# Recurrent attention and routed experts on one core: setup of the first two units in another order

## The chip, the cores and the metric

The kernel runs on one core of a Trainium2 chip. The metric is the device time of one execution in microseconds (us); where several executions are given, it is their median. The core's engines are TensorE (PE in the profile, PEld for its weight loads), VectorE (DVE), ScalarE (ACT), GpSimd (POOL) and SyncE (SP, which here issues the DMAs from and to HBM). Each engine takes its own instructions in the order in which they are written, and waits on semaphores that other engines or DMAs raise.

## The reference

Two stages: a recurrent attention over 4 batches, 8 heads, 768 tokens and head dimension 48, and a layer of 8 experts that takes its 3072 tokens of 384 features, each token going to the one expert with the highest logit.

```python
for t in range(S):                       # attention, per batch and head
    kt, vt, rt = k[:, :, t], v[:, :, t], r[:, :, t]
    cur = np.einsum('bhd,bhe->bhde', u[None] * kt, vt)
    y[:, :, t] = np.einsum('bhd,bhde->bhe', rt, state + cur)
    state = w[None, :, :, None] * state + np.einsum('bhd,bhe->bhde', kt, vt)
...
logits = x @ w_gate + modality_bias[modality_id]      # experts, x is y in token order
e_idx = np.argmax(logits, axis=1)
...
for e in range(E):
    mask = e_idx == e
    h = np.maximum(x[mask] @ w1[e], 0.0)
    out[mask] = gate_w[mask, None] * (h @ w2[e])
```

## The kernel before, in words

The tokens of the attention are cut into 24 units of 128 tokens: 6 chunks of each of the 4 batches, chunk by chunk. Within a unit the recurrence is written as products: with powers of the decay w, the scores of a token against the earlier tokens of its unit are (decayed r) times (decayed keys). For unit i the kernel computes

- `kc`, the keys turned to features by tokens, times powers of w (`keys`, L384), on VectorE;
- `rc`, r times powers of w (`decay`, L359), on GpSimd;
- `rk`, r times the keys, for the bonus u (`own_turned`, L377, on VectorE for units 0 to 3; `own_keys`, L371, on GpSimd later);
- the scores `psc` from `kc` and `rc`, 32 small products on TensorE (`scores`, L424), masked to `at` by VectorE (`causal`, L430);
- `pd`, which for unit 0 is called `psd`, from `rk` and u (`bonus`, L393), copied to `d` (`taken`, L398), and from it `dv` on ScalarE (`own`, L410);
- `kt`, the keys times the last powers (`carry`, L366), on GpSimd, for the state that later chunks take;
- the output `py` and the state's part `pst` on TensorE (`values`, L461 and L474).

r and k come turned from HBM into four buffers `ud`, the keys and values in token order into five buffers `kv`. For units 1 to 12 only r comes turned, and TensorE turns the keys itself (`keys_turned`, L347, tile `pkT`); for these units VectorE reads the keys from PSUM. For unit 0 VectorE reads keys and r from `ud`, in SBUF. The first 16 rows of `ud` are padding and must be blank.

`setup` (L82) prepares unit 0 and part of units 1 and 2 before the loop over the units begins, in an order written out by hand, engine by engine: blanks; the first DMAs; 10 products on constants (`pwarm`); the identity, the mask and counters (`counts`, L245: `base` and `line` are the counters' copies); the powers `pw`, `powk`, `powr`; `w128`, the 128th power; then `rc`, `kc` and `rk` of unit 0, the scores of unit 0, and `wtok`. For `wtok` ScalarE scales `powk` by `w128` (`wk`, L169), TensorE turns the four tiles (`pwk`, L176) and ScalarE copies the result (L177). `kt` needs `wtok`.

Two functions set what follows. `run` (L1090) goes through the units in a loop of steps; step i calls the functions above for the units around i, and a small table (`plan`) hangs further work at the end of a step. `pace` (L350) makes SyncE wait for a value of a running unit before it issues the next unit's transfers.

Of the kernel before, what the change touches and what calls it, by code (L numbers as in the profile page):

```python
# [9 lines left out]
F32 = mybir.dt.float32  # L10
# [50 lines left out]
LOW, TOP = 64 - D, 64 + D  # L61
# [3 lines left out]
class _Kernel:  # L65
# [16 lines left out]
    def setup(self):  # L82

        nc, c = self.nc, self.c
        w = c.tile([P, NPR], F32, name="w")
        nc.vector.memset(w, 1.0)
        nc.sync.dma_start(w[LOW:TOP, :], self.wT.rearrange("j d a -> (j d) a"))
        uT = c.tile([P, NPR], F32, name="uT")
        self.ud = [c.tile([P, 2 * NPR * P], F32, name=f"ud{q}") for q in range(4)]
        self.kv = [c.tile([P, LOW + 2 * DM], F32, name=f"kv{q}") for q in range(5)]  # L90
        self.kt = [c.tile([P, NPR, TOP], F32, name=f"kt{q}") for q in range(4)]
        self.st = [c.tile([P, B, NPR, 2 * D], F32, name=f"st{q}") for q in range(2)]
        zero = c.tile([P, P // 2], F32, name="zero")
# [4 lines left out]
        for t in self.kv:  # L98
            nc.vector.memset(t[:, :LOW], 0.0)
        nc.vector.memset(self.ud[0][:LOW], 0.0)  # L100
        nc.gpsimd.memset(self.ud[1][:LOW], 0.0)
        H2 = P // 2
        blank = lambda t: nc.scalar.copy(t.rearrange("p (a z) -> p a z", z=P // 2), zero[: t.shape[0]].unsqueeze(1).to_broadcast([t.shape[0], t.shape[1] // (P // 2), P // 2]))
        wb, one0, pw = (c.tile([P, NPR, H2 + 1], F32, name=n) for n in ("wb", "one0", "pw"))
        nc.vector.memset(wb, 0.0)
        nc.vector.memset(one0, 0.0)
        nc.vector.memset(one0[:, :, 0:1], 1.0)
        nc.vector.memset(uT, 0.0)
        blank(self.ud[2][:LOW])
        self.turned(0)  # L110
        self.turned(1)
        nc.sync.dma_start(uT[LOW:TOP, :], self.u.rearrange("o (a z) -> z (o a)", a=NPR))
# [35 lines left out]
        powk = self.powk = c.tile([P, NPR, P], F32, name="powk")  # L148
# [3 lines left out]
        nc.scalar.copy(self.powr[:, :, H2:], pw[:, :, :H2])  # L152
        nc.scalar.copy(self.powr[:, :, :H2], powk[:, :, : H2 - 1 : -1])
        self.w128 = c.tile([P, NPR], F32, name="w128")
        p64 = pw[:, :, H2 : H2 + 1].rearrange("p a o -> p (a o)")
        nc.vector.tensor_mul(self.w128, p64, p64)
        self.ub, self.uw = (c.tile([P, NPR, 2], F32, name=n) for n in ("ub", "uw"))
        self.decay(0, NPR, NPR // 2)
        self.keys(0, 2)
        u = self.ctx_[0]  # L160
        nc.vector.tensor_mul(u["rc"][:TOP, NPR // 2 :], u["rT"][:TOP, NPR // 2 :], self.powr[:TOP, NPR // 2 :])
        self.own_turned(0)
        self.decay(1)
        self.scores(0)
        self.wtok = c.tile([P, NPR, 2 * D], F32, name="wtok")
        wk = []
        for pr in range(NPR):
            t = self.a.tile([P, P], F32, tag="wk", name=f"wk{pr}", bufs=4)
            nc.scalar.activation(t, powk[:, pr, :], AF.Copy, scale=self.w128[:, pr : pr + 1])  # L169
            wk.append(t)  # L170
        blank(self.ud[3][:LOW])
        for t in self.kt:
            nc.scalar.copy(t[:, :, :LOW], zero[:, : NPR * LOW].rearrange("p (a z) -> p a z", a=NPR))
        pt = self.ps_y.tile([P, 512], F32, tag="y", name="pwk")
        for pr in range(NPR):
            nc.tensor.transpose(pt[:, pr * P : (pr + 1) * P], wk[pr], id32)  # L176
        nc.scalar.copy(self.wtok, pt.rearrange("p (a z) -> p a z", a=NPR)[:, :, LOW:TOP])  # L177
        blank(self.st[1].rearrange("p b a e -> p (b a e)"))
        nc.gpsimd.memset(self.ub, 0.0)
        for j, r in enumerate(HALVES):  # L180
            nc.gpsimd.tensor_copy(self.ub[r, :, j], uT[r])
        self.keys_turned(1)
        self.causal(0, 0)
        self.causal(0, 1)
        self.keys(1)
        self.own_turned(1)
        self.carry(0)
        self.decay(2)
        nc.gpsimd.tensor_mul(self.uw, self.ub, w.unsqueeze(2).to_broadcast([P, NPR, 2]))
        pst = self.ps_s.tile([P, 512], F32, tag="s", name="psd")  # L190
        self.bonus(0, pst)
        self.taken(0)
        self.carry(1)
        self.feed(3)
        self.turned(4)

# [48 lines left out]
    def counts(self):  # L245

        c, v = self.c, self.nc.gpsimd
        self.onesb = c.tile([P, P], BF16, name="onesb")
        v.memset(self.onesb, 1.0)
        self.id16 = c.tile([P, P], F16, name="id16")  # L250
        make_identity(self.nc, self.id16)
        self.tok = c.tile([P, NT // P], I32, name="tok")
        v.iota(self.tok, pattern=[[P, NCH], [S, B]], base=0, channel_multiplier=1)
        ii = c.tile([P, 3, E], I32, name="idxi")
        for q, (step, base) in enumerate(((1, 0), (-1, E), (CAP, 0))):
            v.iota(ii[:, q], pattern=[[step, E]], base=base, channel_multiplier=0)
        ci = c.tile([P, 3, E], F32, name="idxf")
        v.tensor_copy(ci, ii)
        self.idx, self.rev, self.cbase = (ci[:, q] for q in range(3))
        self.base = c.tile([P, E], F32, name="base")  # L260
        v.tensor_copy(self.base, self.cbase)
        self.line = c.tile([P, 1], F32, name="line")
        v.tensor_copy(self.line, self.tok[:, 0:1])

    def setup5(self):
        nc, c = self.nc, self.c
# [823 lines left out]
    def run(self):  # L1090
        nc, tc, m = self.nc, self.tc, self.m
# [25 lines left out]
        def plan(step, f):  # L1117
            at.setdefault(step, []).append(f)
# [70 lines left out]
        for i in range(NU - 1):  # L1189
# [304 lines left out]
```

## Time and profile before

| | us |
|---|---|
| three runs | 353.38, 355.96, 357.29 |
| median | 355.96 |
| the profiled execution | 353.3 |
| its span, first to last instruction | 351.5 |
| TensorE busy in it | 330.6 (94%) |
| VectorE, ScalarE, GpSimd busy | 220.0, 179.5, 154.6 |

A timeline row gives the start from the span's first instruction, the duration, the engine, the line of the kernel, the operation, what it writes and reads, and in brackets how long the engine sat idle before it and what ended that. Consecutive instructions of one kind stand in one row with their number, and its duration then runs from the first one's start to the last one's end. Instructions of one engine overlap slightly: the next starts some 0.05 to 0.1 us before the end of the one before.

### The profile page before, as it was taken

How to read it: one execution, taken by the hardware profiler on the slowest of the kernel's cores; microseconds unless marked ns; L12 is line 12 of the kernel's file. 1: busy time of each engine (PE TensorE's matmuls, PEld its weight loads, DVE VectorE, ACT ScalarE, POOL GpSimd, SP SyncE). 2: the span in 40 equal slices, each digit the busy share in tenths (PEclk: the TensorE clock that was granted, in tenths of full speed). 3: DMA queues.
4: the chain of work that ended last, by engine and by line, in shares of the span. 5: the costliest groups of instructions: out<-in, count | busy, mean ns of one | idle time of the engine just before them, and what ended most of it. 6: DMA issues, size and time to landing. Idle time of an engine off the chain costs nothing. (4 is left out here: it accounts for less than half of the span.)

```text
span 351.5 us, 15420 instructions
## 1 busy us (share of the span) xinstructions
PE 330.6 (94%) x5555; PEld 269.6 (77%) x5555; DVE 220.0 (63%) x740; ACT 179.5 (51%) x476; POOL 154.6 (44%) x230
## 2 busy tenths in 40 slices
PE   7999998969899997999999999998999999999993
PEld 3888898868768885978888777776778888777771
DVE  6878898799898956498458843348423332334850
ACT  7678776867957644667542222247222224553820
POOL 8888678776646762435265711112111120121221
PEclk9999999878999998999999999999999999999999
DMA  6767677999539998736334632116722111112110
GB/s 194 214 157 166 141 174 214 319 263 211 138 112 195 265 208 235 173 103 122 92 92 137 229 118 64 45 45 207 224 53 59 45 45 45 45 45 67 35 45 5
DMA packets 56798, 46.96 MB, mean 134 GB/s; under 512 B 42920, under 2 KB 50359, under 8 KB 56496
## 3 DMA queue, kind: packets, MB, share of 16 engines
q1 hardware_dynamic: 53552, 36.86, 44.2%
q0 software_dynamic: 3200, 9.47, 7.7%
q8 instruction: 31, 0.51, 0.7%
q14 instruction: 15, 0.12, 0.1%
HBM read 26.03 MB, written 11.83 MB: 108 GB/s over the span
## 5 line engine op out<-in xcount | busy, mean ns | idle before, releaser
L997 PEld LDWEIGHTS <-whi 128*128 128x128 f16 x1248 | 72.4, 98 | 3.6 <-issue 0.9
L1067 PEld LDWEIGHTS <-hh 128*128 128x128 f16 x416 | 38.7, 98 | 29.5 <-ACT hh L1001 3.1
L997 PE MATMUL phb<-mxT,whi 128*128 128x128 f16 x768 | 50.7, 219 | 0.0
L410 ACT ACTIVATE dv<-kv,d 128x48 f32<-128x48 f32 x172 | 43.1, 324 | 2.3 <-POOL gap L664 1.8
L1001 ACT ACTIVATE hh<-phb 128x256 f16<-128x256 f32 (+1 forms) x48 | 21.4, 453 | 32.6 <-PE L997 16.9
L997 PEld LDWEIGHTS <-wlo 128*128 128x128 f16 x624 | 37.7, 98 | 0.0
L371 POOL TENSOR_TENSOR rk<-rc,kc 112x512 f32<-112x512 f32 x20 | 25.7, 1286 | 25.0 <-DVE ebx L309 12.0
L430 DVE TENSOR_TENSOR at<-psc,mask 128x512 f32<-128x512 f32 x48 | 31.7, 682 | 6.0 <-PE psc L424 6.0
L1006 DVE SCALAR_TENSOR_TENSOR hl<-phb,hh 128x256 f16<-128x256 f32 (+1 forms) x48 | 24.1, 511 | 17.5 <-ACTq L1424 15.0
L1087 DVE TENSOR_SCALAR fac<-mt,wf 128x1 f32<-128x1 f32 x17 | 3.6, 213 | 49.1 <-ACTq L1424 36.1
L359 POOL TENSOR_TENSOR rc<-ud,powr 112x512 f32<-112x512 f32 (+1 forms) x25 | 31.1, 1248 | 3.6 <-DMA ud<-in_pd 2.6
L966 POOL TENSOR_TENSOR seenb<-otb,putb 128x1 int32<-128x1 int32 x16 | 3.0, 188 | 65.1 <-ACTq L1424 53.2
L1067 PEld LDWEIGHTS <-hl 128*128 128x128 f16 x208 | 19.8, 99 | 14.7 <-issue 2.4
L424 PE MATMUL psc<-rc,kc 64*64 64x128 f32 (+1 forms) x768 | 29.7, 294 | 1.4 <-POOL rc L359 0.7
L957 ACT ACTIVATE otb<-po,fac 128x384 f32<-128x384 f32 x16 | 9.2, 578 | 41.8 <-PE phb L997 41.8
L665 POOL DMA_INDIRECT rows<-row,posi x24 | 24.9, 1039 | 10.4 <-DVE pr L742 3.3
L1067 PE MATMUL po<-whi,hh 128*128 128x384 f16 x136 | 28.3, 327 | 1.1 <-ACT hh L1001 1.0
L997 PE MATMUL phb<-mxT,wlo 128*128 128x128 f16 x384 | 29.3, 219 | 0.0
L1067 PE MATMUL po<-wlo,hh 128*128 128x384 f16 x136 | 28.0, 326 | 1.3 <-DVE wlo L943 1.3
L424 PEld LDWEIGHTS psc<-rc,kc 64*64 64x64 f32 (+1 forms) x768 | 22.9, 143 | 7.9 <-issue 2.7
L943 DVE SCALAR_TENSOR_TENSOR wlo<-raw,ws,whi 128x1024 f16<-128x1024 f32 (+1 forms) x20 | 27.0, 1389 | 1.2 <-ACT whi L938 1.2
L997 PE MATMUL phs<-mxT,whi 128*128 128x128 f16 x432 | 27.2, 219 | 0.0
(272 smaller groups left out, 663.4 us busy)
## 6 DMA issues: line engine op xcount, KB each, us to landing
kv<-in_pt SPq DMA_DIRECT2D x21, 384.0 KB, 5.5
raw<-in_w SPq DMA_DIRECT2D x12, 512.0 KB, 4.7
ud<-in_pd SPq DMA_DIRECT2D x12, 384.0 KB, 6.0
raw<-in_w SPq DMA_DIRECT2D x2, 1536.0 KB, 6.4
ud<-in_pd SPq DMA_DIRECT2D x12, 192.0 KB, 2.7
rows<-pad SPq DMA_DIRECT2D x10, 193.0 KB, 3.1
kv<-in_pt SPq DMA_DIRECT2D x6, 192.0 KB, 3.7
rows<-row,posi POOLq DMA_INDIRECT x24, 4.5
```

What stands on the lines that cost most here:

```text
L359: nc.gpsimd.tensor_mul(u["rc"][:TOP, s], u["rT"][:TOP, s], self.powr[:TOP, s])
L371: nc.gpsimd.tensor_mul(u["rk"][:TOP], u["rc"][:TOP], u["kc"][:TOP])
L410: nc.scalar.activation(u["dv"][:, sl], u["v"][:, sl], AF.Copy, scale=u["d"][:, h : h + 1])
L424: nc.tensor.matmul(u["ps"][j][s, pr * P : (pr + 1) * P], u["kc"][r, pr, s], u["rc"][r, pr, :], start=True, stop=True)
L430: nc.vector.tensor_mul(u["at"][:, j * NPR : (j + 1) * NPR, :], u["ps"][j].rearrange("p (q t) -> p q t", q=NPR), self.mask.unsqueeze(1).to_ ...
L665: i = nc.gpsimd.indirect_dma_start(out=self.rows, out_offset=bass.IndirectOffsetOnAxis(ap=u["posi"][:, b : b + 1], axis=0), in_=u["row"][: ...
L943: self.nc.vector.scalar_tensor_tensor(self.wlo[:, sl], self.raw[:, sl], sc, self.whi[:, sl], ALU.mult, ALU.subtract)
L957: self.nc.scalar.activation(ot, po[:, :DM], AF.Copy, scale=gf[:, t : t + 1])
L997: self.nc.tensor.matmul(ph[:, q * P : (q + 1) * P], w[:, c0 : c0 + P], self.xT[:, xq, t * P : (t + 1) * P], start=i == q == 0, stop=i == l ...
L1001: self.nc.scalar.activation(self.hh[:, f0 : f0 + fb, t * P : (t + 1) * P], p3, AF.Relu)
L1006: self.nc.vector.scalar_tensor_tensor(self.hl[:, f0 : f0 + fb, r], p3, 0.0, self.hh[:, f0 : f0 + fb, r], ALU.max, ALU.subtract)
L1067: self.nc.tensor.matmul(po[:, :DM], h[:, f, t * P : (t + 1) * P], w[:, c0 : c0 + DM], start=first, stop=last)
```

## The change

In `setup`:

- `rk` of unit 0 moves from VectorE to GpSimd, as GpSimd's first product.
- `rc` of unit 0, of which GpSimd did the first two quarters and VectorE the second half, is now all VectorE's. VectorE does keys and decayed r in two halves, in turn, and `w128` after them.
- GpSimd's copies to `base` and `line` leave the setup for step 3 of the loop (`settle_counts`).
- The blanks of the buffers `ud1` to `ud3` are halved; the other halves are done by GpSimd at the ends of steps 5, 6 and 7 (`blank_rest`). ScalarE's blank of `ud3` is early now; its blanks of `kt` come ahead of `wk`, the blank of the state ahead of the copy to `wtok`.
- TensorE turns unit 1's keys ahead of `pwk`. Unit 0's bonus is written earlier, and its copy to `d` stands ahead of `rk` of unit 1 on VectorE.
- On GpSimd `rc` of unit 2 stands ahead of `kt` of units 0 and 1.
- The blank of `uT` is VectorE's second instruction instead of one behind the other blanks.

```diff
@@ setup
         uT = c.tile([P, NPR], F32, name="uT")
+        nc.vector.memset(uT, 0.0)
...
-        nc.gpsimd.memset(self.ud[1][:LOW], 0.0)
+        nc.gpsimd.memset(self.ud[1][:LOW, : NPR * P], 0.0)
...
-        nc.vector.memset(uT, 0.0)
-        blank(self.ud[2][:LOW])
+        for q in (2, 3):
+            blank(self.ud[q][:LOW, : NPR * P])
...
+        self.ub, self.uw = (c.tile([P, NPR, 2], F32, name=n) for n in ("ub", "uw"))
+        u = self.ctx_[0]
...
+        nc.gpsimd.tensor_mul(u["rk"][:TOP], u["kT"][:TOP], u["rT"][:TOP])
+        for q in range(2):
+            prs = slice(q * NPR // 2, (q + 1) * NPR // 2)
+            nc.vector.tensor_mul(u["kc"][:TOP, prs], u["kT"][:TOP, prs], powk[:TOP, prs])
+            nc.vector.tensor_mul(u["rc"][:TOP, prs], u["rT"][:TOP, prs], self.powr[:TOP, prs])
         p64 = pw[:, :, H2 : H2 + 1].rearrange("p a o -> p (a o)")
         nc.vector.tensor_mul(self.w128, p64, p64)
-        self.ub, self.uw = (c.tile([P, NPR, 2], F32, name=n) for n in ("ub", "uw"))
-        self.decay(0, NPR, NPR // 2)
-        self.keys(0, 2)
-        u = self.ctx_[0]
-        nc.vector.tensor_mul(u["rc"][:TOP, NPR // 2 :], u["rT"][:TOP, NPR // 2 :], self.powr[:TOP, NPR // 2 :])
-        self.own_turned(0)
         self.decay(1)
         self.scores(0)
         self.wtok = c.tile([P, NPR, 2 * D], F32, name="wtok")
+        for t in self.kt:
+            nc.scalar.copy(t[:, :, :LOW], zero[:, : NPR * LOW].rearrange("p (a z) -> p a z", a=NPR))
         wk = []
...
-        blank(self.ud[3][:LOW])
-        for t in self.kt:
-            nc.scalar.copy(t[:, :, :LOW], zero[:, : NPR * LOW].rearrange("p (a z) -> p a z", a=NPR))
+        blank(self.st[1].rearrange("p b a e -> p (b a e)"))
+        self.keys_turned(1)
         pt = self.ps_y.tile([P, 512], F32, tag="y", name="pwk")
...
-        blank(self.st[1].rearrange("p b a e -> p (b a e)"))
...
-        self.keys_turned(1)
+        pst = self.ps_s.tile([P, 512], F32, tag="s", name="psd")
+        self.bonus(0, pst)
         self.causal(0, 0)
         self.causal(0, 1)
         self.keys(1)
+        self.taken(0)
         self.own_turned(1)
+        self.decay(2)
         self.carry(0)
-        self.decay(2)
+        self.carry(1)
         nc.gpsimd.tensor_mul(self.uw, self.ub, w.unsqueeze(2).to_broadcast([P, NPR, 2]))
-        pst = self.ps_s.tile([P, 512], F32, tag="s", name="psd")
-        self.bonus(0, pst)
-        self.taken(0)
-        self.carry(1)
@@ counts
+    def settle_counts(self):
+        v = self.nc.gpsimd
         v.tensor_copy(self.base, self.cbase)
         v.tensor_copy(self.line, self.tok[:, 0:1])
+
+    def blank_rest(self, q):
+        self.nc.gpsimd.memset(self.ud[q][:LOW, NPR * P :], 0.0)
@@ run
+        plan(3, self.settle_counts)
+        for q in (1, 2, 3):
+            plan(4 + q, lambda q=q: self.blank_rest(q))
```

The instructions of VectorE from `powk` to the first mask, before (`ud_85` is unit 0's buffer, `w_184` is `w128`):

```order
L151 TENSOR_TENSOR powk<-pwi_176,pw 128x4x64 [waits DVE_49]
L156 TENSOR_TENSOR w_184<-pw 128x4
L384 TENSOR_TENSOR kc_191<-ud_85,powk 112x256 [waits DMAHW1_49,DVE_49,Activation_49]
L384 TENSOR_TENSOR kc_191<-ud_85,powk 112x256
L161 TENSOR_TENSOR rc_188<-ud_85,powr 112x256 [waits Activation_49]
L377 TENSOR_TENSOR rk_195<-ud_85 112x512
L430 TENSOR_TENSOR at_246<-psc_0_199,mask 128x512 [waits PE_49,Pool_49]
```

and in the changed kernel (line numbers there are its own; `ud_86` is unit 0's buffer, `w_183` is `w128`):

```order
L152 TENSOR_TENSOR powk<-pwi_175,pw 128x4x64 [waits DVE_49]
L164 TENSOR_TENSOR kc_187<-ud_86,powk 112x256 [waits DMAHW1_49,DVE_49,Activation_49]
L165 TENSOR_TENSOR rc_186<-ud_86,powr 112x256 [waits Activation_49]
L164 TENSOR_TENSOR kc_187<-ud_86,powk 112x256
L165 TENSOR_TENSOR rc_186<-ud_86,powr 112x256
L167 TENSOR_TENSOR w_183<-pw 128x4
L442 TENSOR_TENSOR at_252<-psc_0_197,mask 128x512 [waits PE_49,Pool_49]
```

The product `rk` has left VectorE, half of `rc` has come, and `w128` has gone from the front to the back.

GpSimd from the counters' cast to the first `kt`, before (`rc_188` is unit 0's, `rc_197` unit 1's):

```order
L258 CAST idxf<-idxi 128x24 [waits Pool_49]
L261 COPY base<-idxf 128x8 [waits Pool_49]
L263 CAST line<-tok 128x1
L359 TENSOR_TENSOR rc_188<-ud_85,powr 112x128 [waits DMAHW1_49,Activation_49]
L359 TENSOR_TENSOR rc_188<-ud_85,powr 112x128
L359 TENSOR_TENSOR rc_197<-ud_86,powr 112x512 [waits DMAHW2_49]
L179 MEMSET ub 128x8
L181 COPY ub<-uT 64x4 [waits DMAHW3_49,Pool_49]
L181 COPY ub<-uT 48x4
L366 TENSOR_TENSOR kt_94<-kv_89,wtok 128x4x96 [waits DMAHW5_49,Activation_49,Pool_49]
```

and in the changed kernel (`rc_195` is unit 1's, `rc_261` unit 2's):

```order
L262 CAST idxf<-idxi 128x24 [waits Pool_49]
L161 TENSOR_TENSOR rk_188<-ud_86 112x512 [waits DMAHW1_49]
L371 TENSOR_TENSOR rc_195<-ud_87,powr 112x512 [waits DMAHW2_49,Activation_49]
L184 MEMSET ub 128x8
L186 COPY ub<-uT 64x4 [waits DMAHW3_49,Pool_49]
L186 COPY ub<-uT 48x4
L371 TENSOR_TENSOR rc_261<-ud_88,powr 112x512 [waits DMAHW6_49,Pool_49]
L378 TENSOR_TENSOR kt_95<-kv_90,wtok 128x4x96 [waits DMAHW5_49,Activation_49]
```

Two small copies and two quarters of `rc` have left, and `rk` of 512 columns has come as the first product, waiting for the DMA of unit 0 alone.

TensorE behind the scores of unit 0, before:

```order
L176 MATMUL pwk<-id_148,wk_224 128x128 [waits Activation_49]
L347 MATMUL pkT_241<-id_148,kv_90 112x128 [waits DMAHW4_49]
L347 MATMUL pkT_241<-id_148,kv_90 112x128 x3
L393 MATMUL psd<-ub,rk_195 64x2 [waits DVE_49,Pool_49]
L393 MATMUL psd<-ub,rk_195 64x2 x7
```

and in the changed kernel:

```order
L359 MATMUL pkT_229<-id_149,kv_91 112x128 [waits DMAHW4_49,Pool_49]
L359 MATMUL pkT_229<-id_149,kv_91 112x128 x3
L182 MATMUL pwk<-id_149,wk_220 128x128 [waits Activation_49]
L182 MATMUL pwk<-id_149,wk_222 128x128 [waits Activation_49]
L182 MATMUL pwk<-id_149,wk_224 128x128 [waits Activation_49]
L182 MATMUL pwk<-id_149,wk_226 128x128 [waits Activation_49]
L405 MATMUL psd<-ub,rk_188 64x2 [waits Pool_49]
L405 MATMUL psd<-ub,rk_188 64x2 x7
```

The four turns of `wk`, each waiting for ScalarE, now stand behind the turns of unit 1's keys and directly ahead of unit 0's bonus, and the bonus waits for GpSimd alone.

## Rows read from the trace of the kernel before

**Rows 1.** Windows, first units: PE, PEld, DVE, ACT, POOL busy; clock, DMA share, GB/s.
```profile
10.00:15.00 5.00, 5.00 (x116) 4.00 (x116) 4.28 (x9) 3.86 (x12) 4.50 (x5) 1.00 0.86 263
```
**Rows 2.** Timeline of PE, 0 to 16 us: start, duration, what, [idle before].
```profile
1.38 4.45 PE L130 MATMUL pwarm<-warm 128*128 128x512 f16 x10 [1.38 <-POOL warm L96]
6.38 0.71 PE L424 MATMUL psc<-rc,kc 64*64 64x128 f32 x8 [0.55 <-POOL rc L359]
7.25 1.56 PE L424 MATMUL psc<-rc,kc 64*64 64x128 f32 x24 [0.16 <-POOL rc L359]
8.73 1.11 PE L176 MATMUL pwk<-id,wk 128*128 128x128 f32 x4
9.64 0.97 PE L347 MATMUL pkT<-id,kv 128*112 128x128 f32 x4
10.54 0.63 PE L393 MATMUL psd<-ub,rk 112*64 112x2 f32 x16
11.11 0.65 PE L347 MATMUL pkT<-id,kv 128*112 128x128 f32 x4
...
12.33 1.10 PE L424 MATMUL psc<-rc,kc 64*64 64x128 f32 x32
...
14.34 0.57 PE L474 MATMUL pst<-kv,kt 128*64 128x48 f32 x15
```
**Rows 3.** Timeline of DVE, 0 to 16 us.
```profile
4.92 0.76 DVE L384 TENSOR_TENSOR kc<-ud,powk 112x256 f32<-112x256 f32 x2
5.59 0.42 DVE L161 TENSOR_TENSOR rc<-ud,powr 112x256 f32<-112x256 f32 x1
5.93 0.95 DVE L377 TENSOR_TENSOR rk<-ud 112x512 f32<-112x512 f32 x1
...
11.26 0.68 DVE L377 TENSOR_TENSOR rk<-pkT,ud 112x512 f32<-112x512 f32 x1
```
**Rows 4.** Timeline of POOL, short windows from 4.5 us, and 0 to 16 us.
```profile
4.54 0.34 POOL L258 CAST idxf<-idxi 128x24 f32<-128x24 int32 x1
4.95 0.44 POOL L261 COPY base<-idxf 128x8 f32<-128x8 f32 x1
5.34 0.39 POOL L263 CAST line<-tok 128x1 f32<-128x1 int32 x1
5.69 0.64 POOL L359 TENSOR_TENSOR rc<-ud,powr 112x128 f32<-112x128 f32 x1
6.29 0.91 POOL L359 TENSOR_TENSOR rc<-ud,powr 112x128 f32<-112x128 f32 x1
...
8.39 0.10 POOL L179 MEMSET ub<- 128x8 f32 x1
8.55 0.41 POOL L181 COPY ub<-uT 64x4 f32<-64x4 f32 x2
```
**Rows 5.** Lines by form, POOL, 7.3 to 18 us: count | busy us, mean ns | idle.
```profile
L359 POOL TENSOR_TENSOR rc<-ud,powr 112x512 f32<-112x512 f32 x4 | 5.2, 1294 | 0.0
L366 POOL TENSOR_TENSOR kt<-kv,wtok 128x384 f32<-128x384 f32 x4 | 4.1, 1017 | 1.5 <-issue 1.5
```
**Rows 6.** Timeline of ACT, 0 to 16 us.
```profile
4.85 0.40 ACT L153 COPY powr<-powk 128x256 f32<-128x256 f32 x1
5.16 1.27 ACT L169 ACTIVATE wk<-powk,w 128x128 f32<-128x128 f32 x4
...
10.26 1.48 ACT L103 COPY st<-zero 128x1536 f32<-128x1536 f32 x1
```
**Rows 7.** Timeline of POOL, 19.6 to 52 us.
```profile
25.50 1.27 POOL L371 TENSOR_TENSOR rk<-rc,kc 112x512 f32<-112x512 f32 x1 [0.72 <-DVE ebx L309]
...
42.69 1.27 POOL L371 TENSOR_TENSOR rk<-rc,kc 112x512 f32<-112x512 f32 x1 [0.89 <-DVE ebx L309]
```
**Rows 8.** Timeline of POOL, the first us.
```profile
1.27 0.94 POOL L101 MEMSET ud<- 16x1024 f32 x1
```
**Rows 9.** Windows, the first stretch at a lower granted clock; columns as in rows 1.
```profile
61.60:65.00 3.40, 3.15 (x42) 2.55 (x40) 2.61 (x14) 1.91 (x6) 3.17 (x4) 0.50 0.88 284
```

More of the change, by code (lines that the diff above doesn't have):

```diff
@@ L154, in setup @@
         self.w128 = c.tile([P, NPR], F32, name="w128")
+        self.ub, self.uw = (c.tile([P, NPR, 2], F32, name=n) for n in ("ub", "uw"))
+        u = self.ctx_[0]
+        u["rc"] = self.a.tile([P, NPR, P], F32, tag="rc", name="rc0", bufs=4)
+        u["kc"] = self.a.tile([P, NPR, P], F32, tag="kc", name="kc0")
+        u["rk"], u["uw"] = self.a.tile([P, NPR, P], F32, tag="rk", name="rk0"), self.ub
+        nc.gpsimd.tensor_mul(u["rk"][:TOP], u["kT"][:TOP], u["rT"][:TOP])
[3 more added lines that the diff above has]
+            nc.vector.tensor_mul(u["rc"][:TOP, prs], u["rT"][:TOP, prs], self.powr[:TOP, prs])
         p64 = pw[:, :, H2 : H2 + 1].rearrange("p a o -> p (a o)")
         nc.vector.tensor_mul(self.w128, p64, p64)
-        self.ub, self.uw = (c.tile([P, NPR, 2], F32, name=n) for n in ("ub", "uw"))
-        self.decay(0, NPR, NPR // 2)
-        self.keys(0, 2)
-        u = self.ctx_[0]
-        nc.vector.tensor_mul(u["rc"][:TOP, NPR // 2 :], u["rT"][:TOP, NPR // 2 :], self.powr[:TOP, NPR // 2 :])
-        self.own_turned(0)
         self.decay(1)
@@ L260, in counts @@
         self.base = c.tile([P, E], F32, name="base")
+        self.line = c.tile([P, 1], F32, name="line")
+    def settle_counts(self):
+        v = self.nc.gpsimd
         v.tensor_copy(self.base, self.cbase)
-        self.line = c.tile([P, 1], F32, name="line")
         v.tensor_copy(self.line, self.tok[:, 0:1])
+    def blank_rest(self, q):
+        self.nc.gpsimd.memset(self.ud[q][:LOW, NPR * P :], 0.0)
     def setup5(self):
```

## The prediction

> **What bounds the kernel now.** I read the page's busy times first, then the windows, then the timelines of the first 16 us engine by engine. TensorE is the busiest engine, and in the stretch from 10 to 15 us it is busy for all of 5.00 us [rows 1]. Its timeline shows how it comes there [rows 2]: ten products on constants, an idle 0.55 us until GpSimd's first quarter of `rc` is there, eight products, 0.16 us idle for the second quarter, 24 products, and from 8.73 us on each piece starts on the heels of the one before. So what the setup decides is when TensorE's unbroken run begins and whether a hole comes into it. The reader is to see two holes, both ended by GpSimd's `rc`; work that TensorE does not wait for is free.
>
> The same rows show TensorE's level. Ten products of 512 columns take 4.45 us, which is 0.43 us each, the lower level of 1.2 GHz; 24 score products take 1.56 us (65 ns each) at 7.25 us and 32 take 1.10 us (34 ns each) at 12.33 us; the same four turns take 0.97 us at 9.64 us and 0.65 us at 11.11 us [rows 2]. The windows print a clock of 1.00 there [rows 1], so here the level is read from the matmuls: lower until about 10.4 us, upper from then on.
>
> **How VectorE and GpSimd disturb each other.** VectorE starts its products of 256 columns 0.335 us apart ((5.59 - 4.92) / 2), with 0.42 us for one; the unit-0 `rk` takes 0.95 us, where the later `rk` of the same size, which reads PSUM, takes 0.68 us: 0.27 us too long [rows 3]. A GpSimd product takes 1.294 us for 512 columns and 1.017 us for 384, so 128 columns cost 0.277 us, 512 columns 1.11 us, and a lone one of 128 columns would take 1.294 - 3 x 0.277 = 0.46 us [rows 5]. The two of 128 columns beside VectorE's products took 0.64 and 0.91 us, 0.18 and 0.45 us too long [rows 4]. VectorE's excess is just one GpSimd product's columns (0.277 us), and the second excess of GpSimd is about what is left of VectorE's `rk` then. I read this as turns: an engine's whole product waits for the other's whole product, first come first served.
>
> The Trainium skill, page "SBUF — State Buffer", section "SBUF: two separate sides", states such a rule: VectorE and GpSimd share one pair of ports, which is locked by one instruction as a whole, by a VectorE operation with two SBUF inputs only against a GpSimd one that reads SBUF, and the loser blocks. By that rule the change puts two long GpSimd products between four short VectorE ones, and the sum below holds; were the ports shared in proportion, the first rival below would. The excess of 0.27 us agrees with it.
>
> **The scores of unit 0, +0.8 to +1.2 us.** After the change GpSimd asks for `rk` when its cast ends, 4.54 + 0.34 = 4.88 us, or a little earlier [rows 4], VectorE for the first half of `kc` at about 4.92 us [rows 3]. `powr` is complete at 4.85 + 0.40 = 5.25 us [rows 6] and delays nothing. Two GpSimd products (`rk`, `rc` of unit 1) and four halves of VectorE have to take turns: 2 x 1.11 + 4 x 0.335 = 3.56 us from 4.9 us, plus 0.09 us of ending (0.42 - 0.335), so the last half of `rc` is there at 8.55 us in either order. Before, the last piece TensorE waited for was there at 6.29 + 0.91 = 7.20 us. If GpSimd is first, the turns go `rk`, `kc`, `rc` of unit 1, `rc`, `kc`, `rc`, and the first half is ready at 4.9 + 1.11 + 0.335 + 1.11 + 0.335 + 0.09 = 7.88 us; if VectorE is first, at 6.79 us. TensorE starts 0.05 us behind (6.38 against 5.69 + 0.64). At 65 ns each, 32 products from 7.93 us end at 10.0 us; 16 from 8.60 us end at 9.64 us. Before they ended at 7.25 + 1.56 = 8.81 us.
>
> **The turns of `wk`, and what remains: +0.7 us.** The turns of unit 1's keys follow now, some 0.9 us as before (9.64 to 10.54) [rows 2]. Then TensorE waits for `wk`, which waits for `w128`, now VectorE's last. With GpSimd first, GpSimd ends `rc` of unit 1 near 7.6 us, fills and copies `ub` (8.39 to 8.96 before, 0.57 us [rows 4]), asks for `rc` of unit 2 near 8.2 us, ahead of `w128` near 8.46 us, and holds it off until 9.57 us. `wk` takes 1.27 us [rows 6], so from about 9.75 to 11.0 us, its fourth turn starts at 11.05 us, and `psd` at 11.2 to 11.3 us instead of 10.54 us: **+0.7 us**. With VectorE first, GpSimd comes to `rc` of unit 2 behind `w128`, `wk` is early, and `psd` starts 0.4 to 0.8 us late, by where the level rises. I take +0.7 us, since the cast's end lies ahead of 4.92 us. From `psd` on TensorE's pieces stand in the same order and were unbroken, so the shift stays. Bounds of this term: +0.4 and, with the lower level throughout, +1.2 us.
>
> **The parts at nothing.** `kt` of unit 0: the blank of the state (1.48 us [rows 6]) stands ahead of the copy to `wtok` now, so that ends near 12.9 us and `kt` near 13.95 us; its reader starts at 14.34 + 0.7 = 15.0 us [rows 2], 1.1 us of cover. GpSimd's queue behind it (`kt` of unit 1, `rc` of unit 3) comes 1.3 us late and meets its next wait for VectorE some 5 us on, a wait of the kind of rows 7. `base` and `line` (0.44 and 0.39 us, stretched [rows 4]) come ahead of unit 5's `rk`, where GpSimd idled 0.72 us [rows 7]: at worst 0.1 us late, for a bonus that TensorE does at the end of that step. The three halves of blanks cost 0.94 / 2 = 0.47 us each [rows 8], ahead of `rk` of units 7 to 9, with an idle of at least 0.89 us there [rows 7]. `d` a product earlier on VectorE serves `dv` behind ScalarE's blank. The early blank of `uT` lets SyncE issue the first `kv` transfers some 0.5 us earlier; no hole of TensorE in rows 2 was ended by a DMA. Were these covers gone, each would cost its own 0.1 to 0.5 us.
>
> **The sum.** The profiled execution took 353.3 us and lies 2.7 us under the median of the three runs; 353.3 + 0.7 = 354.0 us for it, and on the median 355.96 + 0.7 = **356.7 us**, no measurable change. About 1% (3.6 us) is what a measurement can tell.
>
> **Rivals.** *No turns*: VectorE is not held up, or keeps its turn while its next product is ready. For it: the halves of `kc` beside `base` and `line` were not stretched (0.76 us for two) [rows 3]; but those copies read 8 columns and 1. Against it: the 0.27 us. Then all halves are ready at 4.92 + 4 x 0.335 + 0.09 = 6.35 us, TensorE goes on from 5.83 us without a hole, 32 x 0.065 us bring the scores to 7.9 us, and all that follows is about 1.0 us earlier: 355.0 us. Products that both stretch in proportion (0.95 / 0.68 = 1.4) lie between, at scores about 0.9 us earlier.
>
> *The level rises later*, which ends slower than before. Place: TensorE's hole behind the ten products, 0.55 us before and 1.0 to 2.1 us after. It decides if the rise comes as late behind the new start as behind the old one, or later still. A rise that is x us later costs x / 2, since work takes twice as long at the lower level (65 against 34 ns): by 1.5 us later (7.93 - 6.38) 0.8 us, and by the 3.4 us that the first low stretch lasts [rows 9] 1.7 us. With the shift that is up to +2.4 us: 358.4 us. For it: the rise came after 4 us of nearly unbroken work from 6.38 us. Against it: ten products had run before.
>
> The page "TensorE: Matmul & The Clock Gate" of the Trainium skill, section "What's actually happening", says that the lower level is the default and that sustained work releases it; the drop of the turns from 0.97 to 0.65 us agrees, and by this rule a longer hole speaks for the late rise.
>
> *The shift is absorbed* by a later wait, for data that come at a fixed time: 356.0 us. Little speaks for it, since SyncE's transfers are paced by values of the units and shift along.
>
> **Chances.** Forecast 0.55, no turns 0.2, late rise 0.17, absorbed 0.08. The runs shown lie from 2.6 us under to 1.3 us over their median, so a median can be off by some 1.5 to 2 us. Over +3.6 us: from the forecast 2.9 us are missing (1 in 10), from the late rise 1.2 us (1 in 3): 0.12 in all. Under -3.6 us: 2.6 us are missing from the case without turns (1 in 6), 4.3 us from the forecast (1 in 20): 0.07. The rest, 0.81, is within 1%. The range goes from the case without turns less 1.5 us, 353.5 us, to the late rise plus 1.5 us, 359.9 us; the forecast's own bounds, +0.4 and +1.2 us, lie inside.
>
> **What would show it.** VectorE's four halves stand apart, with one or two of them 1.1 us too long, or all four end by 6.4 us (no turns). The scores end near 9.6 to 10.0 us. The four `wk` turns are preceded by a wait for ScalarE; `w128` is stretched. `psd` starts at 11.0 to 11.3 us. The turns of unit 1's and 2's keys tell by 0.97 or 0.65 us where the level rises. `kt` of unit 0 starts near 12.9 us and the state's products do not wait for it. The forecast is wrong if the scores end before 8.8 us, or if a shift seen at 12 us is not there at 30 us.

## The result and the profile after

The change takes 357.99 us (median of 22 runs, 354.82 to 365.81) beside 353.34 us for before (22 runs): ratio **1.0117, 95% interval 1.0091 to 1.0142**, or 4.1 us. The ratio is taken over each kernel's faster executions (16 of the change's 22; the profiled one is not among them), so it is less than the 4.65 us between the medians. That is slower by a little over 1%, where +0.7 us and no measurable change were forecast. The forecast of 356.7 us lies nearer to 357.99 us than it deserves: it started from 355.96 us, the median of three runs, 2.6 us above that of 22.

The profiled execution took 362.28 us. VectorE's timeline, to set beside [rows 3] (start, duration, what, and in brackets the idle time before it and who ended it):

```profile
5.18 1.52 DVE L164 TENSOR_TENSOR kc<-ud,powk 112x256 f32<-112x256 f32 x1 [0.34 <-DMA ud<-in_pd]
6.62 1.52 DVE L165 TENSOR_TENSOR rc<-ud,powr 112x256 f32<-112x256 f32 x1
8.06 0.41 DVE L164 TENSOR_TENSOR kc<-ud,powk 112x256 f32<-112x256 f32 x1
8.40 0.41 DVE L165 TENSOR_TENSOR rc<-ud,powr 112x256 f32<-112x256 f32 x1
8.73 1.25 DVE L167 TENSOR_TENSOR w<-pw 128x4 f32<-128x4 f32 x1
```

GpSimd's timeline of the same stretch, beside [rows 4]:

```profile
5.12 1.29 POOL L161 TENSOR_TENSOR rk<-ud 112x512 f32<-112x512 f32 x1 [0.23 <-DMA ud<-in_pd]
6.35 1.50 POOL L371 TENSOR_TENSOR rc<-ud,powr 112x512 f32<-112x512 f32 x1
...
8.60 1.36 POOL L371 TENSOR_TENSOR rc<-ud,powr 112x512 f32<-112x512 f32 x1
```

A half that nobody disturbs takes 0.41 us. The first two take 1.52 us, which is 0.41 + 1.11: each waited for one whole GpSimd product, and `w128` of four columns waited for the third. These are the turns of the forecast.

TensorE's timeline, beside [rows 2]:

```profile
1.39 4.45 PE L131 MATMUL pwarm<-warm 128*128 128x512 f16 x10 [1.39 <-POOL warm L97]
8.19 1.98 PE L436 MATMUL psc<-rc,kc 64*64 64x128 f32 x32 [2.36 <-DVE rc L165]
10.11 1.10 PE L359 MATMUL pkT<-id,kv 128*112 128x128 f32 x4
11.00 1.06 PE L182 MATMUL pwk<-id,wk 128*128 128x128 f32 x4
11.99 1.02 PE L405 MATMUL psd<-ub,rk 112*64 112x2 f32 x16
12.94 1.10 PE L359 MATMUL pkT<-id,kv 128*112 128x128 f32 x4
...
15.26 1.99 PE L436 MATMUL psc<-rc,kc 64*64 64x128 f32 x32
17.17 1.33 PE L473 MATMUL py<-kv,at 128*64 128x48 f32 x32
...
19.32 0.65 PE L359 MATMUL pkT<-id,kv 128*112 128x128 f32 x4
```

The reader is to see two things. The hole behind the ten constants products is 2.36 us, not 0.55 us. And TensorE is at its lower level until about 17.6 us, not 10.4 us: unit 1's scores take 1.99 us here and 1.10 us before, and the four turns of `pkT` only come back to 0.65 us at 19.32 us. From `psd` to the start of unit 1's scores there are 3.27 us, before 1.79 us; from there to VectorE's mask of unit 2 (21.70 us, before 17.70 us) 6.44 us, before 5.37 us. So 1.45 us of the shift of unit 2 lie ahead of `psd`, and 2.55 us behind it, with the same pieces in the same order and no hole among them. That is by this pair of profiles; the controls below make another.

Later on this profile is 3.5 us late (units 7 to 12), 5.45 us at the first `po` product (the experts' second product) and 8.81 us at the end. The last 3.4 us are not the change's (see the controls). Nor can the rest be followed to the end in two profiles: between the start and the last 3 us TensorE spends 17.0 us at a granted clock of 0.50 here, 13.6 us in the profile of before, 20.5 us in a second profile of before (c0) and 6.8 us in a second one of the change (c1). So c1 ends 0.8 us earlier than c0, although its unit 2 begins 5.4 us later. What the change costs in all is read from the many executions, and the profiles show where the start loses time.

### The profile page after: what moved, and what is told of

The parts are those of the page before. It is cut to its first block, busy times and chain, and to the rows that moved or that the text cites. A ratio compares the mean times of both kernels' runs of the same rounds, so it can differ in the third digit from the quotient of the medians.

```text
span 360.3 us, 15423 instructions
## 1 busy us (share of the span) xinstructions
PE 336.1 (93%) x5555; PEld 272.9 (76%) x5555; DVE 222.5 (62%) x740; ACT 178.7 (50%) x476; POOL 156.8 (44%) x232
## 3 DMA queue, kind: packets, MB, share of 16 engines
HBM read 26.03 MB, written 11.83 MB: 105 GB/s over the span
## 5 line engine op out<-in xcount | busy, mean ns | idle before, releaser
L1009 PEld LDWEIGHTS <-whi 128*128 128x128 f16 x1248 | 73.5, 99 | 3.9 <-issue 0.8
L1079 PEld LDWEIGHTS <-hh 128*128 128x128 f16 x416 | 37.7, 98 | 35.0 <-ACT hh L1013 8.0
L1018 DVE SCALAR_TENSOR_TENSOR hl<-phb,hh 128x256 f16<-128x256 f32 (+1 forms) x48 | 24.1, 512 | 20.6 <-ACTq L1439 10.2
L436 PE MATMUL psc<-rc,kc 64*64 64x128 f32 (+1 forms) x768 | 31.4, 307 | 2.4 <-DVE rc L165 2.4
L371 POOL TENSOR_TENSOR rc<-ud,powr 112x512 f32<-112x512 f32 x23 | 30.9, 1345 | 3.9 <-DMA ud<-in_pd 2.9
L1079 PE MATMUL po<-whi,hh 128*128 128x384 f16 x136 | 29.3, 328 | 3.2 <-ACT hh L1013 2.3
L436 PEld LDWEIGHTS psc<-rc,kc 64*64 64x64 f32 (+1 forms) x768 | 24.6, 151 | 8.7 <-issue 3.3
L677 POOL DMA_INDIRECT rows<-row,posi x24 | 24.9, 1039 | 10.2 <-DVE pr L754 3.5
L1009 PE MATMUL phs<-mxT,whi 128*128 128x128 f16 x432 | 28.4, 224 | 0.0
L509 ACT ACTIVATE row<-py 128x384 f16<-128x384 f32 x24 | 11.7, 487 | 31.6 <-DVE py L494 29.6
```

Of the source, the lines that this page charges most:

```text
L371: nc.gpsimd.tensor_mul(u["rc"][:TOP, s], u["rT"][:TOP, s], self.powr[:TOP, s])
L436: nc.tensor.matmul(u["ps"][j][s, pr * P : (pr + 1) * P], u["kc"][r, pr, s], u["rc"][r, pr, :], start=True, stop=True)
L509: nc.scalar.activation(u["x16"][:, :DM], u["x"], AF.Square, accum_out=self.grp["ssq"][:, u["at_g"] : u["at_g"] + 1])
L677: i = nc.gpsimd.indirect_dma_start(out=self.rows, out_offset=bass.IndirectOffsetOnAxis(ap=u["posi"][:, b : b + 1], axis=0), in_=u["row"][: ...
L1009: self.nc.tensor.matmul(ph[:, q * P : (q + 1) * P], w[:, c0 : c0 + P], self.xT[:, xq, t * P : (t + 1) * P], start=i == q == 0, stop=i == l ...
L1018: self.nc.vector.scalar_tensor_tensor(self.hl[:, f0 : f0 + fb, r], p3, 0.0, self.hh[:, f0 : f0 + fb, r], ALU.max, ALU.subtract)
```

## The experiments

All ratios are to before, on the same chip. Four kernels ran on each of three chips; before took 353.24 us on the first, 347.52 and 347.54 us on the others. In the expectations T is the theory that the turns make the loss, L that TensorE's longer hole keeps it at its lower level, G that GpSimd's late blanks and copies cost. What they showed, with times in us from each one profile ("hole": TensorE's idle time from the constants products to the last piece of unit 0's scores):

```
kernel                              hole  psd    scores of 1  mask of 2  ratio (95% interval)
before, profile of the prediction   0.71  10.54  12.33        17.70      1
before again (c0)                   0.30   8.96  10.74        16.12      0.9994 (0.9959-1.0030)
the change                          2.36  11.99  15.26        21.70      1.0117 (1.0091-1.0142)
the change again (c1)               2.20  11.83  15.09        21.51      1.0125 (1.0066-1.0185)
change, late parts early (e6)       2.62  11.67  14.94        21.96      1.0118 (1.0062-1.0173)
change, 16 constants products (e1)  1.82  11.61  13.40        18.78      1.0066 (1.0039-1.0093)
change, rk of unit 0 on DVE (e3)    0.81  10.09  12.92        18.87      1.0039 (1.0003-1.0074)
change, rk behind the halves (e5)   0.23  10.07  11.86        17.23      1.0051 (1.0017-1.0085)
e6 with rk behind, uw first (e8)    0.38   8.91  10.70        16.07      0.9968 (0.9931-1.0006)
e8, 12 products, blanks later (e9)  0.08   8.27  10.06        16.60      0.9982 (0.9949-1.0015)
before, late parts only (e4)        0.25   8.79  10.58        17.32      1.0030 (0.9998-1.0062)
before, 12 constants products (e7)  0.25   8.88  10.67        16.04      0.9987 (0.9952-1.0023)
before, 6 constants products (e2)   1.82   9.92  11.72        17.09      1.0117 (1.0067-1.0167)
before, 4 constants products (e10)  2.92  10.16  13.43        19.47      1.0069 (1.0031-1.0107)
```

**The hole filled in the change (e1).** 

> The changed kernel with 16 products on constants ahead of unit 0's scores instead of 10; turns, order and late parts stay. Theory L (TensorE's longer hole behind those products keeps it at the lower level longer, some 3 of the 4.1 us; the turns are worth about 1 us): the hole is nearly filled, unit 1's or 2's key turns show 0.65 us by 12 us, and the time is 0 to 1.5 us over the kernel before. Rival G (GpSimd's late copies and blanks in steps 3 to 7 cost the time): still about 4 us over. Rival T (the turns shift the chain and a later stage multiplies the shift, the level has no part): still about 4 us over, or more.

```diff
-WARM = 10
+WARM = 16
```

TensorE's timeline:

```profile
1.39 4.94 PE L131 MATMUL pwarm<-warm 128*128 128x512 f16 x16 [1.39 <-POOL warm L97]
8.15 1.34 PE L436 MATMUL psc<-rc,kc 64*64 64x128 f32 x32 [1.82 <-DVE rc L165]
...
10.48 1.21 PE L182 MATMUL pwk<-id,wk 128*128 128x128 f32 x4 [0.41 <-ACT wk L176]
...
13.40 1.10 PE L436 MATMUL psc<-rc,kc 64*64 64x128 f32 x32
```

The scores start as in the change (8.15 us), but at the upper level; unit 1's scores start 1.86 us earlier. The 16 products end at 6.33 us, so a hole of 1.82 us is left, and the level outlasts it. But this profile does not show that the six more products brought the level: 16 products take 4.94 us where the change's ten take 4.45 us, and in the trace they start 0.43 us apart up to the seventh and 0.22 us apart from the eighth on. So the level rose here by 4.3 us, in work that the change has too and that ran at the lower level in both of its profiles. What counts for the level in e1 is the total of 12 executions: the ratio falls from 1.0117 to 1.0066 (the two intervals just meet), by which some 1.8 us of the loss would be the level, and about 2.3 us is left for the rest.

**A hole made in before (e2, e10).** 

> The kernel before with 6 products on constants instead of 10, nothing else. They end near 3.9 us, so the hole ahead of the scores at 6.4 us is 2.4 us long, as in the changed kernel, while VectorE's and GpSimd's turns stay as before. Theory L: 2 to 3.5 us slower than the kernel before, the key turns at 0.97 us or more until well after 10.4 us in the profile. Rivals G and T: the same as before, within 1 us.

> The kernel before with 4 instead of 10 products on constants, nothing else: TensorE's hole grows from 0.3 or 0.55 to about 3 us, while the scores of unit 0 begin at the same time as before. Theory L: the level rises several us later, units 1 to 4 begin 2 to 4 us later than in the control, with unit 0 less than 1 us late; ratio 1.008 to 1.015 (6 products gave 1.0117, with a profile whose units were hardly late). Theory T alone (only the order of VectorE and GpSimd costs): ratio 1.000 to 1.003.

```diff
-WARM = 10
+WARM = 6      (e2)
+WARM = 4      (e10)
```

TensorE's timeline of e10, with 4 products:

```profile
1.38 1.89 PE L130 MATMUL pwarm<-warm 128*128 128x512 f16 x4 [1.38 <-POOL warm L96]
6.18 2.15 PE L424 MATMUL psc<-rc,kc 64*64 64x128 f32 x32 [2.92 <-POOL rc L359]
8.27 1.11 PE L176 MATMUL pwk<-id,wk 128*128 128x128 f32 x4
...
13.43 1.77 PE L424 MATMUL psc<-rc,kc 64*64 64x128 f32 x32
```

Fewer instructions, the scores at the same time as in the control (6.18 and 6.13 us), and still unit 2 begins 3.35 us later than there and the kernel is slower by 0.7%. No turn of VectorE and GpSimd was changed, so the late level alone costs time. Two things differ at once, the longer hole and six products fewer ahead of it, and e10 does not tell which of them delays the level; in the change only the hole is longer. The expected ratio (1.008 at least) was a little high. e2 fits worse: its one profile shows the upper level from about 10 us on and units about 1 us late against c0, and the ratio of its six runs is 1.0117. That profile was its shortest run (353.92 us, median 357.04 us); that the level rose later in the others is not shown.

**Late parts alone (e4), and the change without them (e6).** 

> The kernel before with the late parts of the change alone: blanks of three feed buffers halved, their rests by GpSimd behind steps 5 to 7, the two counter copies behind step 3. Theory L and rival T: within 1 us of the kernel before (GpSimd comes to its first product 0.7 us earlier, so the first score may start up to 0.5 us earlier). Rival G: 3 to 4 us slower than before.

> The change without its late parts: the three rest-halves of the blanks are done by ScalarE in the setup, in its idle 4.23 us ahead of `wk`, and `base` and `line` are copied there as before. Theory G (GpSimd's blank at step 6 stands right ahead of its blank of `pad`, and VectorE's small operations of the router wait for both, 1.28 instead of 0.79 us): the loss of 0.45 to 0.5 us between the masks of units 6 and 7 is gone, and the ratio to before falls from 1.0117 to 1.009 to 1.011. Theory L (the long hole of TensorE): the level still rises at about 17 us and units 1 to 4 begin 3.5 to 4 us late. If G and L were both wrong, nothing changes against the change.

```diff
 e4, on before: ud blanked in halves, blank_rest in steps 5 to 7, settle_counts in step 3, as in the change
 e6, on the change:
+        for q in (1, 2, 3):
+            blank(self.ud[q][:LOW, NPR * P :])
...
-        plan(3, self.settle_counts)
-        for q in (1, 2, 3):
-            plan(4 + q, lambda q=q: self.blank_rest(q))
```

The place where G costs is seen in the trace. GpSimd of the change, in the step of unit 6:

```profile
43.94 0.51 POOL L275 MEMSET ud<- 16x512 f32 x1
44.40 0.73 POOL L281 MEMSET pad<- 128x772 int16 x1
```

and VectorE beside it:

```profile
43.88 1.28 DVE L591 TENSOR_SCALAR xinv<-sx 128x4 int32<-128x4 int32 x1
43.95 1.22 DVE L410 COPY d<-pst 128x8 f32<-128x8 f32 x1
```

In e6, where GpSimd has only the blank of `pad` (0.75 us at 44.16 us) there, VectorE:

```profile
44.12 0.82 DVE L585 TENSOR_SCALAR xinv<-sx 128x4 int32<-128x4 int32 x1
```

An operation of four columns ends 0.03 us behind the end of GpSimd's blanks in both. The late blank of `ud` comes in front and holds VectorE's whole queue 0.46 us longer. From the mask of unit 6 to that of unit 7 the change (both profiles), e1, e3, e4 and e5, which have the blank, lose 0.43 to 0.48 us against before, e2 and e6 0.02 us at most. Against the whole, e4 gives +0.3% with an interval that just holds 1, and e6 gives no gain against the change (1.0118, where at most 1.011 was expected): the 0.5 us is shown in its place, and is too small to be shown in the total. Nor is e4's +0.3% the blank's alone: in its profile TensorE waits for unit 2's keys to land, which it does not in c0, and unit 2 begins 1.2 us later than there:

```profile
14.94 0.65 PE L355 MATMUL pkT<-id,kv 128*112 128x128 f32 x4 [1.30 <-DMA kv<-in_pt]
```

e6 shows something else. Here VectorE came first, and half the scores were done at 6.55 us, near the upper level; then TensorE had a hole of 2.18 us:

```profile
5.88 0.67 PE L430 MATMUL psc<-rc,kc 64*64 64x128 f32 x16 [0.44 <-DVE rc L165]
8.73 1.13 PE L430 MATMUL psc<-rc,kc 64*64 64x128 f32 x16 [2.18 <-DVE rc L165]
```

The windows of e6 (busy time of each engine, then the granted clock):

```profile
8.00:10.00 2.00, 1.27 (x17) 0.94 (x18) 0.77 (x3) 1.15 (x4) 1.82 (x5) 0.59 1.16 324
10.00:14.00 4.00, 4.00 (x30) 3.32 (x30) 2.86 (x6) 3.03 (x8) 1.98 (x3) 0.50 0.47 154
14.00:18.00 4.00, 4.00 (x57) 2.83 (x57) 2.08 (x4) 1.06 (x6) 4.00 (x6) 0.50 0.46 152
```

The level that was there is taken back at 8.3 us, in the hole, and given again only at 18.6 us, though TensorE is busy without a break from 8.73 us. So an early rise does not save the start when such a hole follows. The totals of e6 and the change are alike (1.0118 and 1.0117); which engine came first in the executions without a profile is not on record.

**One long product or none beside the halves (e3, e5, e8).** 

> The change with `rk` of unit 0 on VectorE, behind its halves: only one long GpSimd product (`rc` of unit 1) stands between the halves, not two. Theory T+L, by dose: one half is stretched by 1.1 us, the last half is done at about 7.5 us instead of 8.5, TensorE's hole is about 1 us shorter than the change's, and the ratio lies between the variant without any such product (0.997) and the change (1.012): 1.002 to 1.008. If the order of the rest of the setup made the loss, the ratio stays at 1.010 to 1.012.

> The changed kernel with unit 0's r k made by GpSimd as decayed r times keys, so that GpSimd's first product waits for VectorE's last half, and with it the decayed r of unit 1 behind it; the late parts stay. If the products take turns and that opens the hole, VectorE's four halves are 0.34 us apart and done by 6.4 to 6.7 us, TensorE goes from the constants into the scores with a hole under 0.3 us, the scores end near 7.9 to 8.2 us. Theory L then has it 1 to 3 us faster than the kernel before; rival T about 1 us faster; rival G still 3 us slower than before.

> The change without late parts, and without GpSimd beside VectorE's halves: GpSimd fills `ub` and makes `uw` first, then `rk` of unit 0 from VectorE's halves, then `rc` of unit 1. Theory T+L (turns and the long hole made the loss): the four halves take 0.42 us each and are done by 6.7 us, the scores of unit 0 begin near 6.0 us, TensorE's hole is 0.2 us, the level rises by 6 us, and `psd` begins by 9.3 us instead of the 10.07 us of the variant that made `uw` behind `rk`. All units then begin 0.5 to 1.5 us ahead of before, unless a transfer is waited for; ratio 0.996 to 1.003. Theory G alone (the loss is GpSimd's late work only): no more than 0.5 us better than the change, ratio 1.010.

```diff
 e3, on the change: rk of unit 0 by VectorE, behind the halves
-        nc.gpsimd.tensor_mul(u["rk"][:TOP], u["kT"][:TOP], u["rT"][:TOP])
+        nc.vector.tensor_mul(u["rk"][:TOP], u["kT"][:TOP], u["rT"][:TOP])
 e5, on the change: GpSimd makes rk from VectorE's halves, behind them
-        nc.gpsimd.tensor_mul(u["rk"][:TOP], u["kT"][:TOP], u["rT"][:TOP])
+        self.own_keys(0)          # rk = rc * kc
 e8, on e6: as e5, and GpSimd fills ub and makes uw ahead of rk
```

VectorE in e3, with one GpSimd product of 512 columns beside it:

```profile
5.21 0.42 DVE L163 TENSOR_TENSOR kc<-ud,powk 112x256 f32<-112x256 f32 x1 [0.37 <-DMA ud<-in_pd]
5.55 0.42 DVE L164 TENSOR_TENSOR rc<-ud,powr 112x256 f32<-112x256 f32 x1
5.89 1.50 DVE L163 TENSOR_TENSOR kc<-ud,powk 112x256 f32<-112x256 f32 x1
7.31 0.41 DVE L164 TENSOR_TENSOR rc<-ud,powr 112x256 f32<-112x256 f32 x1
```

One product, one stretched half, a last half at 7.72 us, and a ratio between the two ends, as expected by dose. The level has its part here too. It was up at 7.77 us (16 scores in 0.67 us) and was taken back from about 10.7 to 14.1 us, with TensorE busy all the time, so that unit 1's scores took 1.68 instead of 1.10 us:

```profile
12.00:14.00 2.00, 2.00 (x23) 1.16 (x25) 1.03 (x2) 1.53 (x8) 2.00 (x4) 0.50 0.72 201
```

In e8, with none beside it:

```profile
5.04 0.42 DVE L162 TENSOR_TENSOR kc<-ud,powk 112x256 f32<-112x256 f32 x1 [0.21 <-DMA ud<-in_pd]
...
6.06 0.42 DVE L163 TENSOR_TENSOR rc<-ud,powr 112x256 f32<-112x256 f32 x1
```

All four are done by 6.48 us, the hole is 0.38 us, and the whole loss is gone: 0.9968 where the change has 1.0117. By dose of long GpSimd products beside the halves: none 0.9968, one 1.0039, two 1.0117 to 1.0125. e5 has none either and still gave 1.0051; its TensorE shows why the gain of its early scores was lost:

```profile
10.07 0.63 PE L404 MATMUL psd<-uw,rk 112*64 112x2 f32 x16 [1.62 <-POOL uw L186]
```

The place of the wait had moved: `uw` stood on GpSimd behind `rk` and `rc` of unit 1 (1.28 us each). So e5 moves a wait as well as the products, and its ratio does not follow the dose; e8 makes `uw` first.

**Before with a fuller start (e7), and a candidate (e9).** 

> The kernel before with 12 instead of 10 products on constants, which fill TensorE's hole of 0.55 us. Theory L (the hole delays the rise): the level rises by 6 us instead of 10.4, the four turns of unit 1's keys take 0.65 instead of 0.97 us, and unit 1 begins 1 to 2 us earlier; the ratio is 0.995 to 1.000 as far as nothing later takes it back. Theory T (the hole plays no part, only the order of VectorE and GpSimd does): the two more products push the scores back by up to 0.3 us, and the rise stays at about 10 us.

> The candidate for a faster kernel: the variant without GpSimd beside VectorE's halves (0.9968), with 12 products on constants to fill TensorE's hole of 0.38 us, and ScalarE's blanks behind `wk` instead of ahead of it. Theory T+L: the hole is under 0.15 us, the level rises by 6 us, `psd` begins by 8.5 us instead of 8.91, units 1 to 4 begin up to 0.6 us earlier than in that variant; ratio 0.994 to 0.999. If a transfer is waited for behind unit 1, the units begin no earlier and the ratio stays at 0.997.

```diff
 e7, on before, and e9, on e8:
-WARM = 10
+WARM = 12
 e9 also:
-        for q in (1, 2, 3):          # ahead of wk
-            blank(self.ud[q][:LOW, NPR * P :])
...
+        for q in (1, 2, 3):          # behind wk
+            blank(self.ud[q][:LOW, NPR * P :])
```

e7's level is up early (its four turns take 0.60 us at 8.00 us), but the control's was too, and the ratio is 0.9987: no difference. In e9 `psd` starts 0.64 us earlier than in e8, and the gain ends at a transfer:

```profile
14.22 0.65 PE L352 MATMUL pkT<-id,kv 128*112 128x128 f32 x4 [0.72 <-DMA kv<-in_pt]
```

Unit 2 then begins 0.53 us later than in e8, which ran on another chip and waited for no transfer there. Neither e8 nor e9 is shown to be faster than before: both intervals hold 1.

**The controls (c0, c1).** 

> The kernel before, unchanged, as a control for the other runs: every kernel profiled so far (the change and four variants) needs 144.6 to 144.9 us from its first `po` product to the end, the one profile of before 141.2 us. Theory V (the 3.6 us differ from execution to execution): a second profile of before shows about 144.7 us there, and the ratio is 1.000 within 0.003. Theory P (any kernel that is built otherwise loses 3.6 us there): the second profile shows 141 us again.

> The change, unchanged, for a second profile and a time beside the same runs of before as the next three. Theory T+L (turns of VectorE and GpSimd make TensorE's hole, and the hole keeps the lower level longer): the hole is over 2 us again, in whichever order the two engines come, the level rises behind 15 us, unit 2 begins at 21 to 22 us, and the ratio is 1.010 to 1.015. Theory V (the time from the first `po` product to the end is a matter of the chip): 141 or 144.7 us there, the same as the other kernels of this chip. A ratio under 1.006 would say that the loss was a matter of one chip.

No edit: before and the change as they are. TensorE's timeline of before, again:

```profile
6.13 1.58 PE L424 MATMUL psc<-rc,kc 64*64 64x128 f32 x32 [0.30 <-POOL rc L359]
7.64 0.66 PE L176 MATMUL pwk<-id,wk 128*128 128x128 f32 x4
...
8.96 0.63 PE L393 MATMUL psd<-ub,rk 112*64 112x2 f32 x16 [0.22 <-POOL ub L181]
```

The same program has its level up by 7.64 us here and at 10.4 us in [rows 2], with a hole of 0.30 instead of 0.55 us, and its unit 2 begins 1.58 us earlier. So the profile that the prediction rests on had a late rise for its program. The change shows the late level in both of its profiles, and e6 with the other engine first does too; the second one has a hole of 2.20 us and unit 2 at 21.51 us, as T and L together expected, and its ratio is 1.0125 there.

As to the end of the span: from the first `po` product on, all four kernels of the first chip need 144.7 to 144.9 us, and so, nearly, does the first profile of the change (144.6 us); all eight of the other two chips need 141.0 to 141.1 us, the change among them, and the first profile of before 141.2 us. In c0 the second profile of before shows 141 us, as theory P had it and against theory V as it was put there. Theory P then falls by the kernels that are built otherwise and need 141 us too, c1's change among them. What fits every profile is V as c1 puts it: it is a matter of the chip. Which chips the first profiles of before and of the change ran on is not on record. One row of many, ScalarE in the change's first profile,

```profile
223.78 0.38 ACT L1013 ACTIVATE hh<-phb 128x256 f16<-128x256 f32 x1 [1.07 <-PE phb L1009]
```

and the same instruction in c1:

```profile
216.56 0.38 ACT L1013 ACTIVATE hh<-phb 128x256 f16<-128x256 f32 x1 [0.48 <-PE phb L1009]
```

Why ScalarE stands idle 0.6 us longer there is left open.

## Why the prediction was right and wrong

**How VectorE and GpSimd disturb each other: right.** Turns by whole products, 1.11 us of columns each; halves of 1.52 us; the last half ended at 8.81 us against 8.55 us. Nearly all of the 0.26 us is the landing of `ud`, which GpSimd waited for until 5.12 us where 4.9 us was taken; over the profiles VectorE's first half begins anywhere between 4.92 and 5.23 us. The rule of the Trainium skill, page "SBUF — State Buffer", section "SBUF: two separate sides", that the first comer holds the pair of ports for its whole instruction, agrees: 1.52 us is 0.41 + 1.11 us. *No turns* fell.

**The scores of unit 0: right. The wait for `wk`: this step failed.** The scores ended at 10.17 us (9.6 to 10.0 forecast); the landing of `ud` makes up the rest. `w128` was held off for 1.1 us, as forecast, but nothing waited for it. TensorE came to the first `wk` turn at 11.00 us without idle time, straight from the turns of unit 1's keys (in e1, at the upper level, it does wait 0.41 us for `wk`). In c1 `w128` was not held off at all, beside the 1.25 us of the first profile,

```profile
8.57 0.15 DVE L167 TENSOR_TENSOR w<-pw 128x4 f32<-128x4 f32 x1
```

and from the first score to `psd` there are 3.80 us in both profiles (8.19 to 11.99 us, and 8.03 to 11.83 us). So TensorE's own work set `psd`, and the sum had left part of it out: it let TensorE wait for the fourth `wk` turn and counted that turn alone. The four take 0.91 us from start to start in [rows 2] (8.73 to 9.64); behind scores that end at 10.0 us and 0.9 us of key turns they give a `psd` at 11.8 us, where 11.2 to 11.3 us were taken and 11.74 us was the bound. Measured were 11.99 us. The term was +1.45 us and not +0.7 us.

**"From `psd` on ... the shift stays": this step failed.** 2.55 us came on top. It is the rival *the level rises later*, at its place, by its mechanism, but with a chance of 0.17 and a price that was cut short. Its price of half holds if it is counted over the time in which TensorE works at the lower level, not over the delay of the rise (7.2 us): TensorE ran at the lower level from 8.19 to 17.6 us instead of from 6.38 to 10.4 us, 5.4 us longer, and half of that is 2.7 us. What failed, beside the chance, is the cap of 3.4 us on the delay, read off the length of a low stretch in the middle of the kernel [rows 9]; that row says how long one such stretch lasted, not how long a rise can take. The forecast had argued against a late rise from ten products that had run before, with a hole of 1.0 to 2.1 us behind them; in both profiles of the change the rise came late behind such a hole (2.36 and 2.20 us), and in e6 a level already reached was lost behind one of 2.18 us. That the six more products of e1 helped is seen in its total alone. The page "TensorE: Matmul & The Clock Gate", section "What's actually happening", of the Trainium skill says that the start-up varies from run to run of one kernel; the two profiles of before agree, 10.4 us and at most 7.64 us.

**The parts at nothing: one of them was 0.46 us.** `kt`, `base`, `line` and `d` cost nothing, as forecast (`kt` begins at 13.18 us and its reader behind 18 us; `rk` still finds GpSimd idle for 0.47 us behind `base` and `line`). The late blanks did not hold up `rk` either, which was the only thing asked. But VectorE, running beside GpSimd, was held by the one ahead of `pad`. The rule as the forecast gave it, for products with two inputs in SBUF, does not reach a blank. The Trainium skill, page "SBUF — State Buffer", section "SBUF: two separate sides", says also that a VectorE operation in a two-port mode shuts out, or is shut out by, any GpSimd operation; the trace shows the 1.28 us, and does not say which mode `xinv` was in.

**The sum.** On the profile's own time, 1.45 us for the turns and `wk` (with the lower level in them), 2.55 us for the late rise and 0.46 us for the blank make 4.5 us, against 4.1 us by the ratio; the forecast's +0.7 us is the first term alone, and half of it. The split is that of one pair of profiles. From c0 to c1, on another chip, it is 2.87 us ahead of `psd`, 2.52 us behind it and 0.44 us for the blank, 5.8 us in all where the ratio of c1 gives 4.3 us; where the difference is made up is not shown. That 357.99 us lies within the forecast's range, and near the 358.4 us of the late rise, is partly luck, since both were counted from a median 2.6 us too high.

## What to carry to other kernels

Where an engine with two clock levels starts a kernel, price a hole in its first microseconds by all the work that follows at the lower level, and not by the hole; take two profiles of before to see if its level is on the edge. Where two engines take turns by whole instructions, a long instruction beside a chain of short ones costs the chain its full length each time (1.11 us here), and behind the chain it may cost nothing that shows (e8): put it behind, and look who waits for it there (e5). Before a wait is priced, add up what the waiting engine has to do anyway up to that point. When an instruction is moved into an idle stretch of its own engine, look also at what the other engine of the pair does in that stretch.

## What the runs showed of the hardware

- TensorE's level depends on the start in a way that the totals feel: four instead of ten constants products, with the scores at the same time, made the kernel 0.7% slower. When the level rises differs between executions: within the first ten constants products in e1 (by 4.3 us), with the same ten at 10.4 us and at most 7.64 us in before and at 17.6 us in the change.
- A granted clock printed as 1.00 does not say that the upper level was reached: the change's scores take 62 ns each (1.98 us for 32) in such a stretch and 34 ns later. In e6, whose first scores were quicker, the windows print 0.50 for 10.2 us. In e3 a level once reached was taken back at about 10.7 us, with TensorE busy since 7.77 us.
- GpSimd's blanks (0.51 and 0.73 us) hold up a VectorE operation of four columns to their end.
- Chips differ: 3.6 us or more in the same 141 us of the experts, 5.7 us in the median of before.
